# First two slots written from PSUM, relu and squares in tiles of their own, batch 1's softmax on VectorE in a fused three-layer kernel

## The chip, the cores and the metric

One Trainium2 chip, one of its cores. The metric is the device time of one execution in microseconds (us), lower is better; a page of the profile shows one profiled execution and its span. Engines by the names that the profile uses: PE (TensorE, with PEld for its weight loads), DVE (VectorE), ACT (ScalarE), POOL (GpSimd) and SP (SyncE, whose queue issues every DMA of this kernel).

## The reference

Two softmax attentions with shared values, then two feed-forward layers, all in float32.

```
def sm_attn(qq, kk, vv):                      # per batch (8) and head (8), head_dim 64
    a = softmax(qq @ kk.T / sqrt(64))
    return a @ vv
p_packed = sm_attn(p, k, v)                   # 32 packed rows from 576 tokens
x = sm_attn(q, p_packed, p_packed)            # 576 tokens, heads side by side: 512 wide
h = maximum(x @ w_in, 0)                      # 512 -> 2048
y = (h * h) @ w_out                           # 2048 -> 512
h = y @ w_in2                                 # 512 -> 1024
s = h * softmax(h)
out = layernorm(s) * g_ln @ w_out2            # 1024 -> 512, 4608 tokens
```

## The kernel before

Float32 products are made of pieces that TensorE takes at its faster float32r rate: a value is split into `hi` (a cast on ACT) and `lo` (value minus `hi`, on DVE or POOL, the helper `split_lo`), and each product runs as hi·hi, lo·hi and hi·lo.

**Packed attention, t = 0 to 9.** `Pack` handles four batches at once (`K0`: batches 0 to 3; batches 4 to 7 follow inside the main loop). Its results are `L[bg, k]` (packed values, hi and lo) and `slc`.

**The first weight is folded into the packed values.** x @ w_in equals a @ (p_packed @ w_in), head by head. So a `Unit(bg, s, g)` decodes a piece of w_in (s: one of eight column blocks of 512; g: half of the heads), and its `product` multiplies it with `L` for the four batches of group bg, into two PSUM banks named `pw`. ACT and DVE evict them (L320, L321) into the tile `pws`, and `store` writes it to DRAM (`pw_d`), one DMA per batch. `load_slot(b, s)` brings a batch's block back as `slot[b, s]`. For batch 0 and s below 2 there is a shortcut: `store` copies that batch's part of `pws` straight into the slot, four small DMAs per unit (`slot<-pws` in the profile), and three DMAs carry the other batches.

**The second softmax.** `s2_jobs(b, g)` is a list of jobs: scores on PE, 32x32 block transposes on DVE (`t`), row maximum, subtraction (L398), exp on ACT, sum, normalisation (L409), transpose back (`aT`, L414), and the split into `ah` and `al` (`at[b, g]`). `E` names the engine of the subtraction, the normalisation and `al`: DVE for batch 0, POOL for the others. Batch 0's second group runs at t = 9 in two halves of 288 tokens; batch 1 runs in the main loop, steps i = 1 to 5, four jobs in a step from the list `early[1]`, first all of group 0 and then all of group 1.

**The main loop, i = 0 to 255 (t = i + 10).** Step i runs `h1(i)`, six matmuls of a chunk of 128 columns of the first layer for 288 tokens: three with `at[b, 0]`, then three with `at[b, 1]`. ACT makes the relu r; the squares follow twice, once in full (`gg`, on ACT, or on POOL in part of the steps) and once as `hi` (`gh`, on ACT), and DVE makes `lo`: `gl` = gg - gh. Four steps later (three from i = 48) `ymm` runs twelve matmuls of the second product with gh and gl into four PSUM banks `Y`. Steps 0 to 3 and 4 to 7 are batch 0 with `slot[0, 0]` and `slot[0, 1]`; steps 8 to 15 are batch 1. r and gg are the two halves of one tile `rg`, of which there are two in turn:

```
        rg, g2 = t25("1", "rg"), t25("2", "ghl", F32R)
        r, gg, gh, gl = rg[:, :HF], rg[:, HF:S], g2[:, :HF], g2[:, HF:S]
        A.activation(r, pb[:, :HF], AF.Relu)
```

so the relu of step n is the first writer of the tile that step n - 2 used, and waits until all of step n - 2's readers are done, DVE's `gl` too.

**Who sets the order.** PE's matmuls and SP's DMAs are kept in program order (`pin`). DVE, ACT and POOL are ordered by a scheduler that plans ahead, except for the steps 138 to 245 (`strict`), where they too keep the order of the code; in those steps the kernel also decodes the weights of the last two layers (`raw`, `dw`, `op`) and prepares their left operands (`yf`, `yo`), and every ACT, DVE and POOL instruction shows line L53. Each engine runs its own list strictly in order. `later` is a list of DMAs put off to the next step; at the start of each step all of them are issued.

The last two layers run after step 249, by Strassen's scheme, with their own loop.

Of the kernel before, what the change touches and what calls it, by code (L numbers as in the profile page):

```python
# [12 lines left out]
F32R = mybir.dt.float32r  # L13
# [3 lines left out]
ALU = mybir.AluOpType  # L17
# [4 lines left out]
B, H, S, D, NPK = 8, 8, 576, 64, 32  # L22
# [3 lines left out]
HF = S // 2  # L26
# [6 lines left out]
def f(ap):  # L33
    return ap.bitcast(F32)


def build(tc, qT, kT, vP, pT, w_in, w_out, w_in2, w_out2, g_ln, out):
# [6 lines left out]
    pin = tc.keep_in_program_order  # L44
# [10 lines left out]
    V, A, G = Engine(nc.vector), Engine(nc.scalar), Engine(nc.gpsimd)  # L55

    def mm(*a, **k):
        pin(PE.matmul(*a, **k))  # L58
# [4 lines left out]
    def dma(out, in_):  # L63
        pin(SP.dma_start(out=out, in_=in_))
# [11 lines left out]
    pw_d = dr.tile([B, 8, P, 2, 512], F32, name="pw_d")  # L76
# [7 lines left out]
    def bank(name):  # L84
        return ps.tile([P, 512], F32, tag="a", name=name, bufs=4)
# [27 lines left out]
    def t25(k, name, dt=F32):  # L113
        return mp.tile([P, KC * P], dt, tag="e" + k, name=name, bufs=2 if k == "1" else 4)
# [47 lines left out]
    L, s1 = {}, {}  # L162
# [114 lines left out]
    wo, slot = {}, {}  # L277
    T0 = 10
    ring, clock = [0], [0]
    later, soons, lows = [], [], []  # L280
# [8 lines left out]
    class Unit:  # L289
# [14 lines left out]

        def product(self):
            bg, s, g = self.bg, self.s, self.g
            t = [bank("pw") for _ in range(2)]
            for j in range(2):
                c = slice(j * 256, (j + 1) * 256)
                for i, (a, x) in enumerate(((0, 0), (1, 0), (0, 1))):  # L310
                    for hh in range(2):
                        r = slice(64 * hh, 64 * hh + 64)
                        mm(t[hh][:, c], L[bg, 2 * g + j][r, a, :], self.w[r, x, c], start=(i == 0), stop=(i == 2))
            if bg == 0 and s < 2 and (0, s) not in slot:
                new_slot(0, s)
            sb = self.pl.tile([P, 4, 2, 2, P], F32R, tag="pws", name="pws", bufs=2)
            for hh in range(2):
                o = sb.rearrange("p (j h) c l x -> p h j c l x", h=2)[:, hh]
                src = t[hh].rearrange("p (j c x) -> p j c x", j=2, c=2)
                pin(A.copy(o[:, :, :, 0], src))  # L320
                V.tensor_tensor(out=o[:, :, :, 1], in0=src, in1=f(o[:, :, :, 0]), op=ALU.subtract)  # L321
            later.append(lambda: self.store(f(sb.rearrange("p h c l x -> p h (c l x)"))))

        def store(self, sf):
            bg, s, g = self.bg, self.s, self.g
            for b4 in range(4):
                r = slice(32 * b4, 32 * b4 + 32)
                if bg == b4 == 0 and s < 2:
                    o = f(slot[0, s].rearrange("p g c l x -> p g (c l x)"))
                    for h in range(4):  # L330
                        dma(o[32 * h:32 * h + 32, g], sf[r, h])
                else:
                    dma(pw_d[4 * bg + b4, s, :, g].rearrange("(h p) c -> p h c", h=4), sf[r])

    def new_slot(b, s):
        slot[b, s] = big4(ring[0], [P, 2, 2, 2, P], "slot", F32R)
        ring[0] += 1
# [17 lines left out]

    def s2_jobs(b, g, qf=None, parts=1):
        bg, b4 = divmod(b, 4)
        E = V if b == 0 else G
        st = {}

        def j_load():
            if qf:
                st["qf"] = qf
                return
            t = atB["p"].tile([P, 2, S], F32, tag="qf", name="qf", bufs=2)
            dma(t, qT[b, g])
            st["qf"] = [t[:, 0], t[:, 1]]

        def j_mm():
            st["t"] = atA.tile([P, 18, 32], F32, tag="t", name="t", bufs=3)  # L370
            st["mx"], st["sm"] = (atA.tile([P, 18], F32, tag=x, name=x, bufs=2) for x in ("mx", "sm2"))
            pb = [bank("s2") for _ in range(2)]
            for j in range(2):
                for k in range(2):
                    mm(pb[j][64 * k:64 * k + 64, :HF], slc[bg][:, 2 * g + k, b4, :],
                       st["qf"][k][:, j * HF:(j + 1) * HF], start=True, stop=True)
            st["pb"] = pb
            if b < 2:
                j_tr()

        def j_tr():
            for j in range(2):
                V.transpose(out=st["t"].rearrange("p n j -> p (n j)")[:, j * HF:(j + 1) * HF], in_=st["pb"][j][:, :HF])

        def part(p):
            n = 18 // parts
            r = slice(p * n, (p + 1) * n)
            c = slice(p * n * 32, (p + 1) * n * 32)
            t, mx, sm = (lambda: st["t"][:, r]), (lambda: st["mx"][:, r]), (lambda: st["sm"][:, r])

            def over(x):
                return x.unsqueeze(2).to_broadcast([P, n, 32])

            def j_max():
                V.tensor_reduce(out=mx(), in_=t(), op=ALU.max, axis=AX.X)

            def j_sub():
                E.tensor_tensor(out=t(), in0=t(), in1=over(mx()), op=ALU.subtract)  # L398

            def j_exp():  # L400
                A.activation(t(), t(), AF.Exp)

            def j_sum():
                V.tensor_reduce(out=sm(), in_=t(), op=ALU.add, axis=AX.X)
                V.tensor_scalar_add(sm(), sm(), 1e-9)
                V.reciprocal(sm(), sm())

            def j_norm():
                E.tensor_tensor(out=t(), in0=t(), in1=over(sm()), op=ALU.mult)  # L409

            def j_back():
                if p == 0:
                    st["aT"] = atA.tile([P, S], F32, tag="t", name="aT", bufs=3)
                V.transpose(out=st["aT"][:, c], in_=t().rearrange("p n j -> p (n j)"))  # L414

            def j_fin(c):
                def go():
                    if (b, g) not in at:
                        at[b, g] = [atp.tile([P, S], F32R, tag=f"a{x}{g}", name="a" + x, bufs=2) for x in "hl"]
                    hi, lo = at[b, g]  # L420
                    A.copy(hi[:, c], st["aT"][:, c])  # L421
                    soon(lambda: split_lo(E, lo[:, c], st["aT"][:, c], hi[:, c]))
                return go

            fins = [j_fin(c)] if parts == 2 else [j_fin(slice(0, HF)), j_fin(slice(HF, S))]
            return [j_max, j_sub, j_exp, j_sum, j_norm, j_back] + fins

        return [j_load, j_mm] + ([j_tr] if b > 1 else []) + [j for p in range(parts) for j in part(p)]


    gt = {}

    def h1(n):
        b, half, fc = n
        c = slice(half * HF, (half + 1) * HF)
        pb = bank("h1")
        w = slot[b, fc // 2][:, :, fc % 2]
        i = 0
        for g in range(2):
            ah, al = at[b, g]  # L440
            for l, x in ((0, ah), (1, ah), (0, al)):
                mm(pb[:, :HF], w[:, g, l], x[:, c], start=(i == 0), stop=(i == 5))
                i += 1
        rg, g2 = t25("1", "rg"), t25("2", "ghl", F32R)
        r, gg, gh, gl = rg[:, :HF], rg[:, HF:S], g2[:, :HF], g2[:, HF:S]
        A.activation(r, pb[:, :HF], AF.Relu)  # L446
        t = clock[0]

        def squares():
            if t < T0 + 20 or strict[0] and t % 2:  # L450
                A.activation(gg, r, AF.Square)
            else:
                G.tensor_tensor(out=gg, in0=r, in1=r, op=ALU.mult)  # L453
            A.activation(gh, r, AF.Square)

        gt[n] = (gh, gl)
        return squares, lambda: split_lo(V, gl, gg, gh)
# [76 lines left out]
    for b in range(2, B):  # L534
        base = (b - 1) * 32
        js = [s2_jobs(b, g) for g in range(2)]
        first, end = (15, 31) if b == 2 else (3, 26)
# [6 lines left out]
        for s in range(8):  # L544
            i = 16 + 2 * s + 3
            if b == 2:
                i = (17, 19, 21, 23, 25, 31, 33, 35)[s]
            if b == 4:
                i = max(i, 9 + 24 * s // 5)
# [122 lines left out]
    for n in range(8):  # L672
        i = P1 + 1 + PS * n
# [242 lines left out]
    for t in range(max(max(j for j in jobs if j != "first"), T0 + N + LAG - 1) + 2):  # L916
        i = t - T0
        clock[0] = t
        for fn in later:
            fn()  # L920
        later.clear()
        for n in ((0,), (1,), (2,), (3,), (4, 5), (6, 7))[t] if t < 6 else ():
            K0.load_v(n)
        if t + 3 < H:
# [26 lines left out]
        if t == 9:  # L951
            early[0] = s2_jobs(0, 1, q0[1], 2)
            for j in early[0][:2]:
                j()
            products()
            for j in early[0][2:9]:
                j()
            open_b()
            early[1] = s2_jobs(1, 0), s2_jobs(1, 1)
            for x in early[1]:  # L960
                x.pop(0)()
            early[1] = early[1][0] + early[1][1]
        strict[0] = R0 <= i < 246
        sq = None
        if 0 <= i < N:
# [146 lines left out]
```

## Time and profile before

| what | value |
|---|---|
| time, median of 3 runs | 1228.52 us (1227.23 to 1230.28) |
| the profiled execution: its time / its span | 1227.72 us / 1225.9 us |
| PE busy | 1146.4 us (94%) |
| DVE, ACT, POOL busy | 876.5, 662.4, 587.6 us (71, 54, 48%) |
| PE busy in 0 to 100, 100 to 200, 200 to 300 us | 63.52, 88.84, 97.11 us |
| PE busy in 600 to 700 us | 92.50 us, with DVE at 82.97 |

The time of an execution is 1.8 us above its span. PE is the engine with the most work; where its busy share falls, the row of the matmul that comes next says how long PE sat idle and what released it. The granted clock (PEclk) is a share of TensorE's full speed: 1.00 is 2.4 GHz, and the lower level, 1.2 GHz, would read 0.50.

### The profile page before, as it was taken

The page shows a single profiled execution, that of the slowest core. Times are in us where ns is not written, and L with a number is a line of the kernel's source. Part 1 is how long each engine was busy: PE and PEld are TensorE (multiplying, and loading weights), DVE is VectorE, ACT ScalarE, POOL GpSimd, SP SyncE. Part 2 cuts the span into 40 slices and gives each one's busy share as a digit, 9 for nine tenths or more (in the row PEclk, how much of TensorE's full clock was granted, in tenths as well). Part 3 has the DMA queues.
Part 4 walks back from the last instruction along what each step waited for, and adds up shares of the span by engine and source line. Part 5 has one row for each costly group of instructions (what it writes and reads, how often), then busy time and mean ns, then how long its engine had stood idle before and what let it go on. Part 6 is the DMA issues. An engine that isn't in the chain of part 4 may idle for free. (4 is left out here: it accounts for less than half of the span.)

```text
span 1225.9 us, 23705 instructions
## 1 busy us (share of the span) xinstructions
PE 1146.4 (94%) x8556; PEld 1057.7 (86%) x8556; DVE 876.5 (71%) x1688; ACT 662.4 (54%) x1501; POOL 587.6 (48%) x599
## 2 busy tenths in 40 slices
PE   6577899999999999999999899999999999999998
PEld 3366899898999998998998899998888889889897
DVE  4867488745326766578887973257989889889886
ACT  3465555344445555565666665435554655655553
POOL 1133255534225534486865762123744664745743
PEclk9888899999999999999999999999999999999999
DMA  9676697755155799789699799644142143223201
GB/s 332 209 215 189 189 270 246 239 197 204 60 196 147 209 292 291 215 307 356 229 386 337 249 341 366 226 167 150 35 151 82 36 151 101 89 83 108 78 23 48
DMA packets 125541, 239.06 MB, mean 195 GB/s; under 512 B 16880, under 2 KB 44528, under 8 KB 125424
## 3 DMA queue, kind: packets, MB, share of 16 engines
q1 hardware_dynamic: 125424, 237.55, 58.1%
q8 instruction: 67, 1.10, 0.4%
q14 instruction: 50, 0.41, 0.1%
HBM read 144.71 MB, written 91.75 MB: 193 GB/s over the span
## 5 line engine op out<-in xcount | busy, mean ns | idle before, releaser
L58 PE MATMUL Y<-ghl,woh 128*128 128x288 f32 x2048 | 471.1, 306 | 17.0 <-DVE ghl L53 7.2
L58 PEld LDWEIGHTS Y<-ghl,woh 128*128 128x128 f32 x2048 | 350.3, 192 | 32.3 <-DVE ghl L53 8.7
L58 PE MATMUL Y<-ghl,wol 128*128 128x288 f32 x1024 | 307.0, 300 | 0.0
L58 PE MATMUL h<-ah,slot 128*128 128x288 f32 x1024 | 217.2, 301 | 25.9 <-DMA slot<-pws 11.3
L58 PEld LDWEIGHTS Y<-ghl,wol 128*128 128x128 f32 x1024 | 197.2, 193 | 0.0
L822 PE MATMUL o<-wx,ch 128*128 128x256 f32 x1008 | 191.0, 286 | 5.0 <-DVE ys L839 3.0
L1016 POOL TENSOR_TENSOR cl<-raw,ch 128x512 fp32r<-128x512 f32 x100 | 148.2, 1500 | 96.6 <-ACT ch L1015 51.1
L58 PEld LDWEIGHTS h<-ah,slot 128*128 128x128 f32 x1024 | 168.5, 192 | 29.1 <-ACT ah L421 12.9
L453 POOL TENSOR_TENSOR rg<-rg 128x288 f32<-128x288 f32 x128 | 93.2, 729 | 182.5 <-ACT rg L446 171.6
L822 PEld LDWEIGHTS o<-wx,ch 128*128 128x128 f32 x1008 | 159.9, 192 | 11.8 <-DVE ys L839 4.4
L58 PE MATMUL h<-al,slot 128*128 128x288 f32 x512 | 152.6, 298 | 0.0
L822 PE MATMUL o<-wx,cl 128*128 128x256 f32 x504 | 142.9, 286 | 2.4 <-POOL cl L1016 1.9
L67 DVE TENSOR_TENSOR ghl<-rg,ghl 128x288 fp32r<-128x288 f32 x149 | 80.4, 545 | 87.7 <-POOL rg L453 58.8
L446 ACT ACTIVATE rg<-h 128x288 f32<-128x288 f32 x148 | 60.4, 408 | 107.8 <-PE h L58 105.2
L53 DVE TENSOR_TENSOR ghl<-rg,ghl 128x288 fp32r<-128x288 f32 x107 | 75.7, 719 | 51.2 <-ACT ghl L53 26.3
L1015 ACT CAST ch<-raw 128x512 fp32r<-128x512 f32 x126 | 76.8, 623 | 61.6 <-DVE raw L1021 53.8
L53 ACT ACTIVATE rg<-h 128x288 f32<-128x288 f32 x108 | 44.1, 408 | 110.5 <-PE h L58 56.2
L822 PEld LDWEIGHTS o<-wx,cl 128*128 128x128 f32 x504 | 96.0, 191 | 4.8 <-POOL cl L1016 2.9
L58 PEld LDWEIGHTS h<-al,slot 128*128 128x128 f32 x512 | 98.3, 192 | 0.4 <-POOL al L67 0.4
L67 POOL TENSOR_TENSOR ws<-dw,ws 128x512 fp32r<-128x512 f32 x32 | 41.9, 1309 | 98.5 <-ACT ws L298 85.0
L822 PE MATMUL h<-wi,y 128*128 128x512 f32 x312 | 83.5, 402 | 0.4 <-DVE hs L839 0.3
L1021 DVE TENSOR_TENSOR raw<-raw 128x512 f32<-128x512 f32 x70 | 74.2, 1069 | 9.9 <-POOL cl L1016 5.0
(166 smaller groups left out, 2118.0 us busy)
## 6 DMA issues: line engine op xcount, KB each, us to landing
pw_d<-pws SPq DMA_DIRECT2D x124, 256.0 KB, 4.4
slot<-pw_d SPq DMA_DIRECT2D x62, 512.0 KB, 6.1
yc_d<-yo SPq DMA_DIRECT2D x98, 256.0 KB, 6.0
y<-yc_d SPq DMA_DIRECT2D x92, 256.0 KB, 4.3
raw<-w_in SPq DMA_DIRECT2D x40, 512.0 KB, 6.4
raw<-w_out SPq DMA_DIRECT2D x24, 512.0 KB, 6.2
kf<-kT SPq DMA_DIRECT2D x32, 288.0 KB, 5.8
out<-ys SPq DMA_DIRECT2D x72, 128.0 KB, 1.7
```

The costliest lines, as they stand in the source:

```text
L53: return (lambda *a, **k: pin(fn(*a, **k))) if strict[0] else fn
L58: pin(PE.matmul(*a, **k))
L67: eng.tensor_tensor(out=lo, in0=x, in1=f(hi), op=ALU.subtract)
L446: A.activation(r, pb[:, :HF], AF.Relu)
L453: G.tensor_tensor(out=gg, in0=r, in1=r, op=ALU.mult)
L822: PE.matmul(bk, x, w[:, y], start=(i == 0), stop=(i == 3 * nk - 1))
L1015: A.copy(c[n][0], x)
L1016: eng.tensor_tensor(out=c[n][1], in0=x, in1=f(c[n][0]), op=ALU.subtract)
L1021: eng.tensor_tensor(out=out, in0=x, in1=y, op=op)
```

## The change

Five edits in one: (1) a new method `first` computes batch 0's part of a unit for s below 2 by itself, with twelve narrow matmuls into one more PSUM bank `pd`, and ACT and DVE write hi and lo from there into the slot; the four `slot<-pws` DMAs of each of the four units go. (2) The stores put off by `later` are held back during steps 1 to 3 and issued at step 4. (3) Batch 1's subtraction, normalisation and `al` go to DVE. (4) Batch 1's two groups are interleaved in `early[1]`. (5) r and gg get a tile each, for the whole loop, each with two halves in turn.

```
         def product(self):
             bg, s, g = self.bg, self.s, self.g
+            if bg == 0 and s < 2:
+                self.first()
...
-            if bg == 0 and s < 2 and (0, s) not in slot:
-                new_slot(0, s)
...
+        def first(self):
+            s, g = self.s, self.g
+            if (0, s) not in slot:
+                new_slot(0, s)
+            t = bank("pd")[:, :256]
+            for j in range(2):
+                for i, (a, x) in enumerate(((0, 0), (1, 0), (0, 1))):
+                    for hh in range(2):
+                        r = slice(64 * hh, 64 * hh + 64)
+                        mm(t[64 * j + 32 * hh:64 * j + 32 * hh + 32], f(L[0, 2 * g + j][r, a, :32]),
+                           f(self.w[r, x, j * 256:(j + 1) * 256]), start=(i == 0), stop=(i == 2))
+            o, src = slot[0, s][:, g], t.rearrange("p (c x) -> p c x", c=2)
+            pin(A.copy(o[:, :, 0], src))
+            V.tensor_tensor(out=o[:, :, 1], in0=src, in1=f(o[:, :, 0]), op=ALU.subtract)
...
         def store(self, sf):
-            for b4 in range(4):
+            for b4 in range(bg == 0 and s < 2, 4):
                 r = slice(32 * b4, 32 * b4 + 32)
-                if bg == b4 == 0 and s < 2:
-                    o = f(slot[0, s].rearrange("p g c l x -> p g (c l x)"))
-                    for h in range(4):
-                        dma(o[32 * h:32 * h + 32, g], sf[r, h])
-                else:
-                    dma(pw_d[4 * bg + b4, s, :, g].rearrange("(h p) c -> p h c", h=4), sf[r])
+                dma(pw_d[4 * bg + b4, s, :, g].rearrange("(h p) c -> p h c", h=4), sf[r])
...
-        E = V if b == 0 else G
+        E = V if b < 2 else G
...
-        rg, g2 = t25("1", "rg"), t25("2", "ghl", F32R)
-        r, gg, gh, gl = rg[:, :HF], rg[:, HF:S], g2[:, :HF], g2[:, HF:S]
+        if not rg:
+            rg.extend(t25("1", "rg") for _ in range(2))
+        g2 = t25("2", "ghl", F32R)
+        c = slice(rn[0] * HF, rn[0] * HF + HF)
+        rn[0] ^= 1
+        r, gg, gh, gl = rg[0][:, c], rg[1][:, c], g2[:, :HF], g2[:, HF:S]
...
-        for fn in later:
-            fn()
-        later.clear()
+        if not 1 <= i <= 3:
+            for fn in later:
+                fn()
+            later.clear()
...
-            early[1] = early[1][0] + early[1][1]
+            x, y = early[1]
+            early[1] = x[:4] + [j for z in zip(x[4:], y) for j in z] + y[len(x) - 4:]
```

The edits move instructions on the engines that a scheduler orders. First VectorE at t = 9, batch 0's second group (tiles `t` and `aT` of 288 columns, two halves). Before:

```order
L398 TENSOR_TENSOR t<-t,mx 128x288
L405 TENSOR_SCALAR sm_694<-sm_694 128x9
L406 RECIPROCAL sm_694<-sm_694 128x9
L409 TENSOR_TENSOR t<-t,sm_694 128x288
L404 TENSOR_REDUCE sm_694<-t 128x9
L414 STREAM_TRANSPOSE aT<-t 128x288
L321 TENSOR_TENSOR pws<-pw,pws 128x2x2x128
```

With the change:

```order
L409 TENSOR_TENSOR t<-t,mx 128x288 x2
L321 TENSOR_TENSOR pws<-pw,pws 128x2x2x128 x2
L141 TENSOR_SCALAR dw<-dw 128x512
L415 TENSOR_REDUCE sm_705<-t 128x9
L147 SCALAR_TENSOR_TENSOR dw<-raw,dw 128x512
...
L149 SCALAR_TENSOR_TENSOR dw<-raw,dw 128x512
...
L420 TENSOR_TENSOR t<-t,sm_705 128x288 x2
L425 STREAM_TRANSPOSE aT<-t 128x288 x2
```

The first half's transpose back (`aT`) now stands behind two `pws` evictions, a decode of three instructions (`dw`) and the second half's own work; before it stood ahead of them.

Next VectorE in steps 2 to 5, batch 1 (576 columns). Before, its last pieces there:

```order
L404 TENSOR_REDUCE sm_925<-t 128x18
L405 TENSOR_SCALAR sm_925<-sm_925 128x18
L406 RECIPROCAL sm_925<-sm_925 128x18
L67 TENSOR_TENSOR ghl<-rg,ghl 128x288
L414 STREAM_TRANSPOSE aT<-t 128x576
```

With the change, from the sum of the first group to the end of the second:

```order
L415 TENSOR_REDUCE sm_905<-t 128x18
L409 TENSOR_TENSOR t<-t,mx 128x576
...
L420 TENSOR_TENSOR t<-t,sm_905 128x576
L415 TENSOR_REDUCE sm_938<-t 128x18
...
L425 STREAM_TRANSPOSE aT<-t 128x576
...
L67 TENSOR_TENSOR al<-aT,ah 128x288 x2
...
L420 TENSOR_TENSOR t<-t,sm_938 128x576
...
L425 STREAM_TRANSPOSE aT<-t 128x576
```

The subtraction, the normalisation and `al` now stand in VectorE's own list, and the second group's steps follow the first group's at one place instead of a softmax later.

Last ScalarE in the strict steps, with the engines that an instruction waits for in brackets (names with h are step outputs in PSUM). Before:

```order
L53 ACTIVATE rg<-h_6359 128x288 [waits DVE_49,PE_49]
L53 ACTIVATE t<-t 128x576
L53 ACTIVATE ghl<-rg 128x288 [waits Activation_49]
L53 ACTIVATE rg<-h_6385 128x288 [waits DVE_49,PE_49]
L53 ACTIVATE t<-t 128x576 [waits Pool_49]
L53 ACTIVATE rg<-rg 128x288 [waits Activation_49]
```

With the change:

```order
L53 ACTIVATE rg<-h_6265 128x288 [waits PE_49,Pool_49]
L53 ACTIVATE t<-t 128x576
L53 ACTIVATE ghl<-rg 128x288 [waits Activation_49]
L53 ACTIVATE rg<-h_6290 128x288 [waits PE_49]
L53 ACTIVATE t<-t 128x576 [waits Pool_49]
L53 ACTIVATE rg<-rg 128x288 [waits DVE_49,Activation_49]
```

The order is the same; the relu (`rg<-h`) waits for VectorE no more, and in the steps where ACT makes the full square (`rg<-rg`) that wait now stands there, behind the instructions in between.

## Rows read from the trace of the kernel before

**Rows 1.** The page, part 1: busy time, share and instructions of each engine.
```profile
PE 1146.4 (94%) x8556; PEld 1057.7 (86%) x8556; DVE 876.5 (71%) x1688; ACT 662.4 (54%) x1501; POOL 587.6 (48%) x599
```

**Rows 2.** PE's waits in 0 to 250 us: total, times, longest.
```profile
PE h L58 <- DMA slot<-pws: 11.3, 2, 6.9
...
PE h L58 <- ACT ah L421: 5.6, 1, 5.6
```

**Rows 3.** PE's waits in 250 to 870 us.
```profile
PE Y L58 <- DVE ghl L53: 7.2, 4, 2.4
PE Y L58 <- ACT ys L53: 4.6, 3, 2.2
```

**Rows 4.** Busy us by stretch: PE, PEld, DVE, ACT, POOL, PEclk, DMA share, GB/s.
```profile
50.00:60.00 10.00, 5.01 (x26) 2.99 (x26) 9.45 (x22) 4.48 (x11) 2.54 (x2) 0.67 0.39 132
60.00:70.00 10.00, 7.63 (x50) 6.15 (x51) 8.49 (x17) 6.76 (x15) 2.60 (x2) 0.65 0.47 113
70.00:80.00 10.00, 5.58 (x31) 4.58 (x30) 3.09 (x6) 3.56 (x9) 2.31 (x2) 0.86 0.83 197
80.00:90.00 10.00, 8.86 (x59) 7.99 (x57) 8.27 (x12) 7.32 (x19) 4.51 (x4) 0.97 0.90 333
90.00:100.00 10.00, 4.92 (x23) 4.10 (x24) 8.75 (x13) 5.61 (x14) 6.20 (x6) 0.55 0.36 121
```

**Rows 5.** Timeline of PE: start, duration, instruction, idle before it and its releaser.
```profile
61.90 0.82 PE L58 MATMUL h<-ah,slot 128*128 128x288 f32 x2 [6.89 <-DMA slot<-pws]
...
76.77 0.50 PE L58 MATMUL h<-ah,slot 128*128 128x288 f32 x2 [4.42 <-DMA slot<-pws]
...
95.03 0.85 PE L58 MATMUL h<-ah,slot 128*128 128x288 f32 x2 [5.61 <-ACT ah L421]
...
137.96 0.82 PE L58 MATMUL h<-ah,slot 128*128 128x288 f32 x2 [5.14 <-DMA slot<-pw_d]
```

**Rows 6.** Timeline: transposes back of the second groups, batch 0 (first half) and batch 1.
```profile
56.79 0.47 DVE L414 STREAM_TRANSPOSE aT<-t 128x288 f32<-128x288 f32 x1
...
93.74 0.78 DVE L414 STREAM_TRANSPOSE aT<-t 128x576 f32<-128x576 f32 x1 [1.04 <-POOL t L409]
```

**Rows 7.** Timeline, 40 to 95 us: durations of the kinds that are added or moved.
```profile
42.17 0.75 DVE L398 TENSOR_TENSOR t<-t,mx 128x576 f32<-128x576 f32 x1
...
53.45 0.98 PE L58 MATMUL pw<-ws,L 64*128 64x256 f32 x12
...
59.98 0.68 DVE L147 SCALAR_TENSOR_TENSOR dw<-raw,dw 128x512 uint32<-128x512 uint32 x1
...
62.89 2.93 PE L58 MATMUL pw<-ws,L 64*128 64x256 f32 x24
...
89.19 1.65 DVE L149 SCALAR_TENSOR_TENSOR dw<-raw,dw 128x512 uint32<-128x512 uint32 x1
...
92.53 1.17 POOL L409 TENSOR_TENSOR t<-t,sm 128x576 f32<-128x576 f32 x1 [2.24 <-DVE sm L406]
```

**Rows 8.** Timeline of SP: the loads of batch 1's first two slots.
```profile
80.40 1.47 SPq L64 DMA_DIRECT2D slot<-pw_d  x2
```

**Rows 9.** ACT's wait of the strict steps in total; timeline of the strict steps.
```profile
ACT rg L53 <- DVE ghl L53: 51.4, 27, 4.2
...
561.63 0.30 PE L58 MATMUL h<-al,slot 128*128 128x288 f32 x1
...
564.70 0.41 ACT L53 ACTIVATE rg<-h 128x288 f32<-128x288 f32 x1 [3.87 <-DVE ghl L53]
...
567.67 0.40 PE L58 MATMUL Y<-ghl,woh 128*128 128x288 f32 x1 [2.25 <-ACT ys L53]
...
658.11 0.40 PE L58 MATMUL Y<-ghl,woh 128*128 128x288 f32 x1 [0.81 <-ACT ys L53]
...
686.34 0.54 PE L58 MATMUL Y<-ghl,woh 128*128 128x288 f32 x2 [2.25 <-DVE ghl L53]
```

**Rows 10.** Stretch behind the wait at 567.67, columns as in rows 4.
```profile
570.00:580.00 10.00, 10.00 (x68) 8.89 (x67) 7.37 (x14) 4.63 (x12) 4.40 (x6) 0.89 1.02 362
```

More of the change, by code (lines that the diff above doesn't have):

```diff
@@ L431, in build @@
     gt = {}
+    rg, rn = [], [0]
     def h1(n):
```

## The prediction

> **What bounds the kernel now.** I read the page first: PE is busy 94% of the span [rows 1], so a gain has to come out of the 80 us in which PE does not work, or out of matmuls that run at the lower clock. Then PE's waits, for two stretches. Up to 250 us the largest are 11.3 us for `slot<-pws`, two waits, and 5.6 us for batch 1's `ah` [rows 2]: both stand where the change edits. From 250 to 870 us PE waits 7.2 us for DVE's `gl` and 4.6 us for ACT's copies of Y [rows 3]: the stage that edit 5 reaches. Then the timeline at these waits [rows 5, 9], and the stretches around them for what else was busy [rows 4]. What the reader is to see there: from 50 to 60 us DVE is busy 9.45 of 10 us while PE idles half the time, from 70 to 80 us DVE has 3.09 us of work, and from 80 to 100 us it is full again. So the start is bound in turn by DVE (softmax of batch 0), by the small DMAs (steps 0 to 4), and by DVE with POOL (softmax of batch 1). PEclk is 0.65 at 60 to 70 us and 0.55 at 90 to 100 us: half of PE's idle time is paid a second time, since behind each long wait matmuls run at 1.2 GHz.
>
> All sums are made against the profiled execution: 1227.72 us, 0.8 us below the median of the three runs.
>
> **The start, step by step.**
>
> (a) *The wait of 6.89 us before 61.90.* Taking away the DMA alone would start PE earlier, since batch 0's first half of `aT` is transposed at 56.79 [rows 6]. But DVE's new list puts other work ahead of that transpose: two `pws` evictions of about 0.66 us each (such an eviction of 128x512 is like the decode op's 0.68 [rows 7]), the three decode ops (two at 0.68, one shorter, 0.4 estimated), the second half's sum and normalisation (288 columns, about 0.45 each, from 0.75 for 576 [rows 7] less a fixed part), small ops (0.35), and the new slot eviction (0.4, estimated as 256 columns against 512 at 0.66; bounds 0.3 and 0.66). That is 1.32 + 1.76 + 0.9 + 0.35 + 0.4 = 4.7 us, so `aT` ends at 57.26 + 4.7 = 62.0 instead of 57.26. PE's 24 narrow matmuls of the units (0, 0) and (0, 1) come on top: twelve `pw` matmuls take 0.98 us [rows 7], the narrow ones stream as many columns and I give them the same; the first twelve push batch 0's scores back by up to 1 us, the second twelve lie in PE's idle time. With the cast, PE resumes between 62.4 and 63.4 instead of 61.90. I take **+1.0 us** (0 to +2): the DMA's wait becomes a wait for DVE, and nothing is won here.
>
> (b) *24 more narrow matmuls* for the units (1, 0) and (1, 1), between step 0 and step 1. The 24 `pw` matmuls there take 2.93 us [rows 7], at PEclk 0.65; at full clock twice 0.98. I take **+2.9 us** (2.0 to 4: one more bank per unit out of four can make PE wait for an eviction, of which the nearest row is 0.66). Eviction itself is four ACT copies and four DVE subtractions of about 0.4 us, counted in (a) and (d).
>
> (c) *The wait of 4.42 us before 76.77* [rows 5]. Step 4 reads `slot[0, 1]`, which DVE now writes right behind the narrow matmuls, some 7 us earlier. **-4.4 us**, and behind it some 3 us at half clock (PEclk 0.86 at 70 to 80, 0.97 at 80 to 90 [rows 4]: 1.4 + 0.3 = 1.7 us lost), of which I take back 1.5. Step 8 would then be reached at its old place, about 88.8, + 1.0 + 2.9 - 4.4 - 1.5 = 86.8 us.
>
> (d) *The wait of 5.61 us before 95.03* for batch 1's second `ah`. Here the end is set by DVE's own list, which I add up from the end of batch 0's `aT` (62.4 to 63.4) to the end of batch 1's second `aT`. With 0.45 us for a `gl` or `al` of 288 columns, 0.48 for a block transpose of 288, 0.75 for 576 columns [rows 7], 0.68 for a decode op and 0.66 for an eviction: behind batch 0's softmax three decode ops, two `al`, one `gl` 3.2; four slot and `pws` groups 3.4; four block transposes 1.9; two maxima, subtractions, sums, normalisations 6.0; small ops 0.9; two `aT` 1.6; `al` 0.9; seven `gl` 3.2; six decode ops 3.6. Sum 24.7 us, so 87 to 88, and 1 to 2 us of waits for ACT's exp: `aT` ends at 88.5 to 90, against 93.74 + 0.78 = 94.5 before [rows 6]. Before, DVE had only 3.09 us of work from 70 to 80 us [rows 4], and behind that the chain took turns with POOL (the 1.17 us of L409 [rows 7], then the transpose). PE resumes at about 90 instead of 95.03: **-5.0 us** in all for (a) to (d), since PE, there at 86.8 + 0.6, waits for this anyway; (a), (b) and (c) are hidden in it as long as they bring PE there before 90. Bounds: if DVE gains nothing on POOL, 0; if its list runs without a gap, -6.5. A shorter wait (2.6 us) should leave less at half clock: 4.5 us are lost at PEclk 0.55 [rows 4], I take **-0.5**.
>
> Perfetto Trace Analysis in the Trainium skill (section Optimizing Scalar/DVE Operations) speaks against this edit: it advises moving work away from a saturated DVE, to GpSimd if need be, and adds that moving work between these two might not help because they share a port. The trace shows the sharing (a decode op of 0.68 us takes 1.65 at 89.19, while POOL runs) and so speaks for taking POOL's part away; by the page's rule alone term (d) would be 0, and the sum -4.5.
>
> (e) *The held-back stores and the loads behind them.* Per unit, SP issues three DMAs instead of seven. Batch 1's two slot loads went out at 80.40 [rows 8]; now four loads of weights and six stores stand ahead of them, the stores waiting for the last `pws` eviction (about 70, from the sum in (d)). At the 0.6 to 0.9 us per issue of SP's rows (1.47 for two [rows 8]) the loads go out at about 75. Step 8 needs them at 87, the cover is 12 us: 0. If that cover is gone, step 8 waits for the slot as step 18 does now (5.14 us [rows 5]).
>
> (f) *Behind 95 us.* Step 18's wait of 5.14 us hangs on a chain of product, store and load that moves along with PE: 0 (bounds -2 and +1).
>
> Start: -5.5 us, bounds -9 and +1.
>
> **Relu and squares apart.** Over the strict steps ACT waits 51.4 us in 27 places for DVE's `gl` of two steps before [rows 9]; ACT is not the bound, so what counts is where PE stood still behind it. At 564.70 a relu had waited 3.87 us; the last of PE's matmuls that it reads ended at 561.63 + 0.30 = 561.9 [rows 9], some 2.7 us earlier. ACT then works from 564.70 to the Y copies, and PE waits for these 2.25 us, until 567.67. With the relu freed the copies come 2.7 us earlier, and the whole wait goes: -2.25. PEclk behind it is 0.89 for 10 us [rows 10]: 1.1 us. The wait of 0.81 at 658.11 is of the same kind: -0.8. At 686.34 [rows 9] PE waits 2.25 us for DVE itself, whose list an earlier ACT can only shorten where it waits for ACT: I take -0.4, near the lower end. The other waits of this kind in [rows 3] count 0. Sum **-4.5 us**. Bounds: 0, if POOL's or ACT's full square, which now does the waiting, is late enough to bring the same waits back; and -11.8, both totals [rows 3], with some 4 us of clock behind them. Nothing can be later than before by this edit alone: each wait that is added was part of one that it replaces.
>
> **Sum.** 1227.7 - 5.5 - 4.5 = 1217.7; forecast **1218 us**.
>
> **The rivals.**
>
> *Half of it: only one of the two gains comes* (either the start is no better, because DVE ends batch 1 at 94 us as before, or the relu's wait only moves on to the square). For it: each rests on chains in which DVE is near full. 1222 to 1224 us. Chance 0.14.
>
> *More: both, and the later waits shrink as well.* In the strict steps a DVE that gets its operands earlier is also ahead at the waits for `gl`. With the bounds above, -9 and -9: 1205 to 1213. Chance 0.12.
>
> *No change.* The waits move on by one: 87 to 95 us filled by DVE, step 18's load later by what the start gained, the strict steps bound by DVE. 1225 to 1231. Chance 0.15.
>
> *Slower: VectorE becomes the bound of the first steps.* It takes over 4.8 us of POOL's work in a stretch where it is already at 8 to 9 tenths. Its price: the list in (d) has some 24.7 us; if a third of it runs at the 1.65 of the decode op beside POOL instead of 0.68, that is +11 us, batch 1 ends at 100, step 8 runs 5 us later than now, and with no gain behind 500 us the time is 1232 to 1234. It decides from the point where the second `aT` ends behind 94.5 us by more than the strict steps give back, about 99. Against it: POOL loses the eight ops of this softmax, so less runs beside DVE. Chance 0.09.
>
> **Chances and range.** Both gains about as summed (1213 to 1222): 0.50; the rivals as above. A measurement tells 0.3%, 3.7 us, from no change: faster 0.50 + 0.14 + 0.12 = 0.76, same 0.15, slower 0.09. The range 1209 to 1229 leaves out the lower half of "more" (0.06) and the upper end of "no change" with "slower" (0.13).
>
> **What would show it.** (a) PE's step 0 resumes at 62 to 64 us, released by ACT's `ah` and not by a DMA. (c) No wait before step 4. (d) The second `aT` of batch 1 ends at 88 to 90 us, and PE's first long wait behind 70 us ends at about 90. (e) The loads of batch 1's slots are issued at 74 to 77 us. Edit 5: ACT's waits for DVE's `gl` at relus vanish, those of the squares take at most half of the 51.4 us, and the waits at 567 and 658 are gone. The prediction is wrong if batch 1's `ah` comes after 94 us, if step 1 stalls for PSUM by more than 3 us, or if PE's total for `gl` and Y copies stays near 11.8 us.

## The result, and the profile after

| what | before | changed kernel |
|---|---|---|
| time, median of 4 runs each | 1227.88 us | **1216.45 us** (1212.41 to 1216.89) |
| ratio to before, 95% interval | | 0.9898 [0.9883, 0.9913] |
| span of the profiled execution | 1225.9 us | 1215.1 us |

The forecast was 1218 us, faster by over 0.3%: both held. The number came out well, in part by luck: of the reasons one was wrong, one edit was taken to be worth nothing and is worth something, and two terms were sized badly; the experiments below sort them. (One of the twelve executions of a kernel further down, the one with the interleave alone, took 2771.84 us, over twice the others, and is in no ratio.)

The page of the changed kernel, part 1, against [rows 1]:

```profile
PE 1148.2 (94%) x8652; PEld 1055.3 (87%) x8652; DVE 879.2 (72%) x1700; ACT 665.6 (55%) x1505; POOL 581.8 (48%) x591
```

PE has 96 more instructions and no less work, so the gain is idle time and clock, as it had to be. PE's waits in 0 to 250 us (total, times, longest), against [rows 2]:

```profile
PE h L58 <- ACT ah L432: 10.1, 2, 6.7
...
PE h L58 <- DMA slot<-pw_d: 4.4, 1, 4.4
```

The 11.3 us for `slot<-pws` are gone, but the waits for `ah` grew from 5.6 to 10.1 us. PE's timeline shows where, against [rows 5]:

```profile
62.50 0.85 PE L58 MATMUL h<-ah,slot 128*128 128x288 f32 x2 [6.68 <-ACT ah L432]
...
89.73 0.53 PE L58 MATMUL h<-ah,slot 128*128 128x288 f32 x2 [3.38 <-ACT ah L432]
...
91.64 0.61 PE L58 MATMUL h<-al,slot 128*128 128x288 f32 x1 [1.38 <-DVE al L67]
...
132.56 0.82 PE L58 MATMUL h<-ah,slot 128*128 128x288 f32 x2 [4.43 <-DMA slot<-pw_d]
```

Step 0 waits as long as before, with ACT's `ah` (and behind it DVE's `aT`) in the DMA's place. Step 4 waits no more. Batch 1's second `ah` lets PE go at 89.73 instead of 95.03. Then `al` is a new wait of 1.38 us. Busy us by stretch, columns as in [rows 4]:

```profile
70.00:80.00 10.00, 10.00 (x77) 8.18 (x78) 8.81 (x21) 7.62 (x18) 0.00 (x0) 1.00 0.88 240
80.00:90.00 10.00, 6.62 (x48) 6.19 (x46) 10.00 (x18) 9.08 (x26) 2.58 (x2) 1.00 0.28 95
90.00:100.00 10.00, 8.12 (x47) 6.94 (x47) 6.97 (x11) 4.73 (x11) 2.97 (x3) 0.66 0.25 87
```

From 70 to 80 us PE and DVE are full, or nearly, where they had 5.58 and 3.09 us of work. From 80 to 90 us DVE is busy 10.00 of 10 us, while POOL works 2.58 us: POOL's idle engine beside DVE's full one is the first hint of what was wrong in the reasons.

How far the change is ahead can be read off SP's stores of `y_d`, which follow the main loop. The first is issued at 252.10 before and at 247.53 after (4.6 us ahead), the one at 525.94 at 521.28 (4.7), the one at 745.25 at 734.50 (10.75), and the end is 10.8 us earlier. So the start gave 4.6 us and the strict steps 6.1; the last two layers nothing.

The strict steps: ACT's wait for `gl` in 500 to 850 us, against [rows 9], and PE's waits in 250 to 870 us, against [rows 3]:

```profile
ACT rg L53 <- DVE ghl L53: 4.5, 5, 2.1
```

```profile
PE Y L58 <- DVE ghl L53: 6.5, 4, 2.7
PE Y L58 <- DVE ys L53: 2.6, 2, 2.3
```

The 51.4 us of ACT are 4.5, and the 4.6 us that PE waited for ACT's Y copies have no row any more.

### The profile page after: what moved, and what is told of

It is laid out like the page before. It is cut to its first block, busy times and chain, and to the rows that moved or that the text cites. A ratio compares the mean times of both kernels' runs of the same rounds, so it can differ in the third digit from the quotient of the medians.

```text
span 1215.1 us, 24017 instructions
## 1 busy us (share of the span) xinstructions
PE 1148.2 (94%) x8652; PEld 1055.3 (87%) x8652; DVE 879.2 (72%) x1700; ACT 665.6 (55%) x1505; POOL 581.8 (48%) x591
## 5 line engine op out<-in xcount | busy, mean ns | idle before, releaser
L58 PE MATMUL h<-ah,slot 128*128 128x288 f32 x1024 | 215.7, 299 | 18.4 <-ACT ah L432 10.1
```

## The experiments

Each kernel is one of the two with one part changed. In the expectations, theory A is the prediction's account and the others are the rivals to it; the last three runs were made after the first eight, and name their theories themselves. What they move is read at two places: when PE resumes for batch 1's second `ah` (95.03 before, 89.73 after), and the first store of `y_d` (252.10 and 247.53). These are of one profiled execution each; a ratio is over several executions, against the kernel before, run beside it.

How far two such executions can differ by themselves is seen at step 0, which none of the edits to batch 1's softmax (3 and 4) is meant to reach. PE resumes there at 61.90 in the kernel before and at 60.28 in the one with the interleave alone, and at 60.76 to 63.79 in the nine kernels with slots from PSUM. A difference of 1 to 2 us at the first store is therefore not shown by one execution; where step 0 is off by as much, it is said. DVE, ACT and POOL are ordered by the scheduler anew for each kernel, so that an edit can move instructions elsewhere too; no run here holds their lists fixed.

### Relu and squares: one tile, and apart alone

The changed kernel with r and gg in one tile again:

```
-        r, gg, gh, gl = rg[0][:, c], rg[1][:, c], g2[:, :HF], g2[:, HF:S]
+        r, gg, gh, gl = rg[:, :HF], rg[:, HF:S], g2[:, :HF], g2[:, HF:S]
```

> The changed kernel with edit 5 undone: relu and full square share a tile again. Theory A (freed relus shorten ACT's and so PE's waits in the strict steps): it loses the 6.2 us that the changed kernel gains between 490 and 780 us, so about 1222.5 (1220 to 1224), with PE's wait for the Y copies near 565 us back and ACT waiting tens of us for DVE's gl at relus. Rival (the strict steps gained because everything reaches them earlier, not through the tiles): 1216 to 1218, and the lead over the kernel before still grows from 4.6 to 10.8 us.

Measured: 1223.14 us, ratio 0.9962 [0.9949, 0.9975]. ACT waits 51.8 us in 27 places for `gl` again. The stores of `y_d` stand 4.3 us ahead of before at the first one and 4.1 at the one at 745.25: the start's gain is kept and nothing is added.

The kernel before with edit 5 alone:

> The kernel before with edit 5 alone. Theory A: the start is as before, the strict steps gain 6 us, about 1221.5 (1220 to 1224). Rival: no change, 1226 to 1229.

Measured: 1221.56 us, 0.995 [0.9938, 0.9961]. The first store is at 251.54 (0.6 us ahead), the last one at 737.40 (7.9 ahead). Theory A's number: edit 5 is worth about 6 us by itself, and it and the start add up.

### Batch 1's softmax: on which engine, in which order

The changed kernel with `E = V if b == 0 else G` (edit 3 undone):

> The changed kernel with edit 3 undone: batch 1's subtraction, normalisation and al on POOL again, interleaved and with the slots from PSUM. Theory A (the start's end is set by the chain to batch 1's second transpose): the chain gets POOL's 1.17 us instead of 0.75 for two steps in each group and a hand-over at each, and al takes 1.0 instead of 0.4 us: PE resumes 2 to 4 us later than 89.7, about 1219 (1217.5 to 1221). Rival B (the start's gain comes from the slots written from PSUM): 1216 to 1217.5.

Measured: 1214.14 us, 0.9897 [0.9883, 0.9911]: not slower, and below either theory's range. PE's timeline, and the stretch of 80 to 90 us:

```profile
87.35 0.53 PE L58 MATMUL h<-ah,slot 128*128 128x288 f32 x2 [0.62 <-ACT ah L432]
```

```profile
80.00:90.00 10.00, 7.90 (x57) 7.14 (x55) 9.97 (x14) 8.35 (x24) 8.03 (x8) 1.00 0.28 97
```

With the softmax on POOL, PE resumes 2.4 us **earlier** than with it on DVE. DVE is still full in this stretch and POOL is busy 8.03 of 10 us: the two groups' chains run side by side on two engines. Theory A fails here.

The changed kernel with `early[1] = early[1][0] + early[1][1]` (edit 4 undone, still on DVE):

> The changed kernel with edit 4 undone: batch 1's groups one after the other, on DVE. Theory A: group 1 gets to DVE one to two steps later, its transpose ends 2 to 5 us behind 89.2, about 1219.5 (1218 to 1222). Rival B: 1216 to 1217.5.

Measured: 1216.92 us, 0.9909 [0.9896, 0.9922].

```profile
93.97 0.85 PE L58 MATMUL h<-ah,slot 128*128 128x288 f32 x2 [5.99 <-ACT ah L432]
```

PE resumes 4.2 us later, as theory A has it, but the time lies in rival B's range and cannot be told from the change's 0.9898. In this execution PE was late already at step 0 (63.79 against 62.50).

Both edits undone (slots from PSUM, stores held and edit 5 stay):

> The changed kernel with edits 3 and 4 undone: slots from PSUM, stores held, r and gg apart, batch 1's softmax on POOL and its groups in turn. If the interleave is what gains the start (first theory): PE resumes at 96 to 98 behind a wait of 8 us or more, and the time is that of edit 5 alone, 1221 to 1222.5 us. If the held stores already bring the softmax forward by themselves (second theory): PE resumes at 92 to 93, 1218.5 to 1220 us.

Measured: 1222.56 us, 0.9948 [0.9929, 0.9967], that of edit 5 alone. The first theory's numbers.

```profile
96.83 0.85 PE L58 MATMUL h<-ah,slot 128*128 128x288 f32 x2 [9.62 <-ACT ah L432]
```

The four together, all with the other edits in:

| batch 1's softmax | step 0 | PE resumes | first `y_d` | median |
|---|---|---|---|---|
| POOL, groups in turn | 62.47 | 96.83 | 254.27 | 1222.56 |
| DVE, groups in turn | 63.79 | 93.97 | 249.78 | 1216.92 |
| POOL, interleaved | 62.71 | 87.35 | 245.63 | 1214.14 |
| DVE, interleaved (the change) | 62.50 | 89.73 | 247.53 | 1216.45 |

Read by the first store, DVE in place of POOL gives 4.5 us while the groups run in turn (5.8 counted from step 0), which fits a chain that need not change engines. The interleave gives 8.6 us on POOL (8.9 from step 0). On top of the interleave, DVE costs 1.9 us (2.1). On DVE the interleave gives 2.3 us, of which only 1.0 are left when counted from step 0. The medians of the last two rows don't tell them apart (the intervals of their ratios are nearly the same); a pair further down does.

The kernel before with the interleave alone:

```
-            early[1] = early[1][0] + early[1][1]
+            x, y = early[1]
+            early[1] = x[:4] + [j for z in zip(x[4:], y) for j in z] + y[len(x) - 4:]
```

> The kernel before with edit 4 alone (batch 1's two groups interleaved, still on POOL, slots by DMA, stores not held, r and gg in one tile). If the interleave alone brings the second `ah` forward (first theory): PE resumes about 90 instead of 95.03, the store of the first y_d at about 249 instead of 252.10, 1225 to 1226.5 us. If the interleave needs the slots from PSUM and the held stores (second theory): the two waits of about 7 and 4.5 us before 77 stay and the slot loads at about 80 end last, PE resumes at 92 or later, 1227 to 1229 us.

Measured: 1225.32 us, 0.9976 [0.9964, 0.9988], as the first theory has it. PE's timeline:

```profile
75.30 0.82 PE L58 MATMUL h<-ah,slot 128*128 128x288 f32 x2 [4.57 <-DMA slot<-pws]
...
88.02 0.50 PE L58 MATMUL h<-ah,slot 128*128 128x288 f32 x2 [0.76 <-ACT rg L446]
```

The two DMA waits stay, yet the wait for batch 1's second `ah` is gone, and the first store is 3.8 us ahead (248.28). Of these, 1.6 us were there before the interleave could act, since step 0 began that much earlier (60.28 against 61.90):

```profile
60.28 0.82 PE L58 MATMUL h<-ah,slot 128*128 128x288 f32 x2 [6.11 <-DMA slot<-pws]
```

That leaves 2.2 us, and 2.6 is what the medians show. So the interleave gains on POOL and without the slots too, though less than the 8.6 us that it gives with slots from PSUM and held stores.

### Slots and held stores

The changed kernel without the hold (`if not 1 <= i <= 3:` taken out):

> The changed kernel with edit 2 undone: the stores of the units (1, 0) and (1, 1) are issued at step 1, ahead of four loads of weights. Theory A: the loads go out some 5 to 9 us later (behind the last pws eviction at 72.8), but they are decoded only from step 4 on: 1216 to 1218, no change. Rival (the hold is what keeps the decode on time): DVE's decode and with it batch 1's second transpose move back by 3 us or more, 1219 to 1222.

Measured: 1218.01 us, 0.992 [0.9903, 0.9937]. SP's timeline, and PE's:

```profile
57.61 18.28 SPq L64 DMA_DIRECT2D pw_d<-pws  x9
75.94 1.16 SPq L64 DMA_DIRECT2D raw<-w_out  x1
```

```profile
92.87 0.53 PE L58 MATMUL h<-ah,slot 128*128 128x288 f32 x2 [3.40 <-ACT ah L432]
```

SP issues in order. Not held, the stores stand in its queue from 57.61 until the last `pws` is evicted, and the loads of weights behind them go out from 75.94 to 78.85, where the change issues them from 59.11 to 65.02. ACT's decode op of such a load stands ahead of its exp of the second group, and waits for the load; DVE waits 1.81 us behind it:

```profile
82.01 0.66 ACT L136 ACTIVATE dw<-raw 128x512 f32<-128x512 f32 x1 [1.78 <-DMA raw<-w_out]
```

`ah` comes 3.1 us later than in the change. Of these, DVE was 1.3 us behind before that wait (the second group's maximum at 77.72 against 76.44), where PE had a lower clock from 60 to 70 us (0.53 against 0.67); the kernel with r and gg in one tile, whose stores are held, had the same (0.54) and resumed at 90.84. So some 1.8 to 2.0 us are the hold's. The first store is at 251.29, 3.8 us behind the change, and 2.5 us are left at the store of 734.50. The rival's mechanism is seen, but the time lies at theory A's upper end, and its interval overlaps that of the change: in the time, the hold's worth is not shown.

The changed kernel with slots by DMA and no hold (edits 1 and 2 undone):

> The changed kernel with edits 1 and 2 undone: batch 0's slots go through pws and DMAs again, batch 1's softmax stays on DVE and interleaved. Theory A: a wait of some 4 us before step 4 comes back, but the chain on DVE to batch 1's second transpose still decides: DVE has 1.7 us less to do, PE 4 us of narrow matmuls less, so 1216 to 1219. Rival B (the slots are what gains): the start's whole gain goes, 1220.5 to 1222.

Measured: 1220.76 us, 0.9939 [0.9922, 0.9957]; first store 249.79. The waits of step 0 and step 4 are back (6.88 and 4.52 us), and PE resumes at 90.43, but now for batch 1's slot:

```profile
90.43 0.50 PE L58 MATMUL h<-ah,slot 128*128 128x288 f32 x2 [1.71 <-DMA slot<-pw_d]
```

Theory A's time is missed; rival B's is met, though by the first store half of the start's lead is still there (2.3 of 4.6 us). With the runs above, this sorts what the start needs, all with edit 5 in:

| slots from PSUM, stores held | softmax on DVE, interleaved | ratio to before |
|---|---|---|
| no | no | 0.995 [0.9938, 0.9961] |
| yes | no | 0.9948 [0.9929, 0.9967] |
| no | yes | 0.9939 [0.9922, 0.9957] |
| yes | yes (the change) | 0.9898 [0.9883, 0.9913] |

Neither pair of edits alone gains anything that its interval shows; both together gain 0.5%. PE needs its own way to step 8 and batch 1's `ah` to come earlier, and whichever is left late sets the time.

The kernel before with slots from PSUM alone (edit 1):

> The kernel before with edit 1 alone: slots from PSUM, no hold, softmax of batch 1 on POOL and in turn, one rg tile. Theory A: the wait before step 4 goes, and PE then waits longer for batch 1's second ah: 1226 to 1229. Rival B: 1222 to 1224.5.

Measured: 1229.11 us, 1.001 [0.9997, 1.0023]. Step 4 no longer waits, and step 8 waits for all of it:

```profile
96.77 0.85 PE L58 MATMUL h<-ah,slot 128*128 128x288 f32 x2 [9.86 <-ACT ah L432]
```

A transfer taken off the path gained nothing by itself here, since a later wait (for `ah`) then took all of the time.

### Beyond the change

The changed kernel with batch 0's fourth slot (s = 3) from PSUM as well, so that step 18's wait for its load has nothing to wait for:

```
-            if bg == 0 and s < 2:
+            if bg == 0 and s in (0, 1, 3):
                 self.first()
...
-            for b4 in range(bg == 0 and s < 2, 4):
+            for b4 in range(bg == 0 and s in (0, 1, 3), 4):
...
-        if i:
+        if i and s != 3:
```

> The changed kernel with one edit more: the slot [0, 3] from PSUM too, for the wait of 4.43 us before 132.56. Its cost is 24 narrow matmuls, 2 us at full clock, and four evictions of 0.4 us. If that wait goes with the half-clock stretch behind it (PEclk 0.66 at 130 to 140, about 3 us) and no wait for PSUM takes its place: 1211 to 1214. If step 18 only waits for the next thing (the evictions of pw, or batch 0's slot 2): 1215 to 1219.

Measured: 1214.0 us, 0.9887 [0.987, 0.9904]. The wait of 4.43 us at 132 is gone; new waits of 0.50, 1.31 and 0.85 us, for a relu and for evictions, stand between 113 and 119. First store 244.29, 3.2 us ahead of the change. The intervals of the two ratios overlap, so the times alone do not show this gain.

The same with the softmax on POOL:

> The changed kernel with batch 1's softmax back on POOL and slot [0, 3] taken from PSUM too. If the two gains are of different places and add (first theory: 2.3 us from POOL by the run with the softmax on POOL, 2.5 us from the slot by the run with the third slot): 1211 to 1212.5 us, PE resumes for batch 1's second `ah` at about 87.4 and no wait of 4 us for the load of slot [0, 3] at about 130. If both gain the same time, which a later wait then takes back (second theory): 1213.5 to 1214.5, and a wait for an eviction between 110 and 150 that neither run alone shows.

Measured: **1209.5 us** (1208.44 to 1210.21), 0.9841 [0.9824, 0.9858], the fastest version here and better than either theory's number. PE resumes at 87.91, and the waits between 113 and 119 are those of the run before. Against that run, which has the softmax on DVE, the intervals do not overlap: with the groups interleaved, POOL is the better place, by 0.46%.

That it gives more than the sum of the two is for the most part the clock. The stretches of 110 to 140 us with the softmax on POOL and two slots from PSUM, and then with three:

```profile
110.00:120.00 10.00, 7.58 (x48) 7.24 (x49) 7.06 (x13) 5.87 (x13) 2.68 (x3) 0.83 0.83 254
120.00:130.00 10.00, 6.51 (x49) 6.27 (x47) 5.82 (x11) 6.74 (x17) 2.56 (x2) 0.94 0.97 274
130.00:140.00 10.00, 8.75 (x51) 8.78 (x52) 2.71 (x5) 4.84 (x13) 0.31 (x1) 0.72 0.53 195
```

```profile
110.00:120.00 10.00, 7.34 (x67) 5.81 (x66) 6.95 (x11) 5.83 (x14) 3.22 (x3) 1.00 0.79 247
120.00:130.00 10.00, 10.00 (x77) 10.00 (x76) 6.86 (x12) 7.94 (x22) 1.95 (x2) 1.00 0.97 265
130.00:140.00 10.00, 10.00 (x81) 9.70 (x80) 5.59 (x11) 7.05 (x18) 3.89 (x4) 1.00 0.51 186
```

With two slots the clock falls to half twice, from 115 us on and from 129. The second fall begins inside the wait that ends at 131.25, where it costs nothing, as the stretch of 129 to 130 shows (PE busy 0.00, PEclk 0.50):

```profile
129.00:130.00 1.00, 0.00 (x0) 0.00 (x0) 0.00 (x0) 0.00 (x0) 0.00 (x0) 0.50 1.03 371
```

Counted only where PE works, 1.7 us of full speed are lost behind 115 and 2.2 behind 131; with three slots nothing is lost from 110 to 140. The waits of 2.42 (for `pws` at 115.11) and 4.74 us (for the load at 131.25) go; 2.7 us of waits between 113 and 119 and 48 narrow matmuls (two units, 2.15 + 1.95 = 4.1 us) come: 2.4 + 4.7 + 3.9 - 2.7 - 4.1 = 4.2 us. Measured are 5.0, from 1.5 us behind at a matmul of Y (99.56 against 98.07) to 3.5 ahead at another (169.03 against 172.53). The lead at the first store is 6.0 us (239.67 against 245.63): from 172 us on another 0.9 come from a wait for a relu that shrinks (1.02 to 0.17), and 1.7 from the clock at 220 to 230 us (0.83 with two slots, 1.00 with three). With three slots and the softmax on DVE such drops remain (0.91 and 0.92 at 110 to 130, 0.83 at 220 to 230), which only the two edits together avoid. Of the 6.0 us, 3.4 are left at the end of the span. The clock's part is read from one execution of each kernel.

## Why the prediction was right, and where it was not

**(a), the wait at 61.90.** Right. DVE's new list was summed to end `aT` at 62.0, and PE to resume at 62.4 to 63.4 behind ACT's `ah`. The changed kernel's DVE and PE: both halves' transposes end at 61.52 + 0.83 = 62.35, and PE resumes at 62.50. The difference from before is +0.6 us (+1.0 predicted), less than step 0 moves by itself between executions.

```profile
61.52 0.83 DVE L425 STREAM_TRANSPOSE aT<-t 128x288 f32<-128x288 f32 x2
```

**(b), the narrow matmuls.** Mis-sized. I counted twelve instructions to a unit, as the code writes them; the trace has 24 to a unit (96 for four units). The operands go through `f`, as plain float32, where the `pw` matmuls are float32r; that this is why was not tried. The two units between step 0 and step 1 took 3.21 and 1.95 us, 5.2 in place of 2.9. It did not show in the sum, since PE still got to step 8 early enough to wait (at 89.73 - 3.38 = 86.35, predicted 86.8).

**(c), the wait at 76.77.** Right: gone, and PEclk is 1.00 from 70 to 90 us.

**(d), the wait at 95.03.** The number was right, the reason wrong. `aT` was to end at 88.5 to 90 and PE to resume at about 90; it ended at 88.45 + 0.76 = 89.2, and PE resumed at 89.73. Even this sum came out by two errors that cancel: from 62.35 to 89.21 us DVE works 22.8 us, not 24.7, and waits 4.1 us, not 1 to 2, nearly all of it before 72.7 us for ACT's halves of the evictions and for `gh`, and not for exp. Further, I put this down to DVE doing POOL's part, so that the chain no longer "took turns with POOL", and gave as bounds 0 if DVE gains nothing on POOL and -6.5 if its list runs without a gap. With POOL doing its part, interleaved, PE resumes at 87.35: 7.7 us earlier than before, beyond the better bound. The step that failed is that I summed DVE's list for the two edits together and never for edit 4 alone. With the softmax on POOL, the second group's maximum comes at 85.85 on DVE in turn, and at 76.55 interleaved:

```profile
85.85 0.74 DVE L406 TENSOR_REDUCE mx<-t 128x18 f32<-128x576 f32 x1
```

```profile
76.55 0.74 DVE L406 TENSOR_REDUCE mx<-t 128x18 f32<-128x576 f32 x1
```

The gap between engines that I saw in [rows 6] was the consequence of one chain alone on two engines, and a second chain fills it.

I also wrote that (a), (b) and (c) are hidden in (d). The table of the section on the slots shows that (d) needs them: with the softmax edits but without slots and hold, the ratio is 0.9939 against 0.995 for edit 5 alone, and the intervals overlap.

The rule of the Trainium skill that the prediction set against this edit (Perfetto Trace Analysis, Optimizing Scalar/DVE Operations) was borne out in part. Interleaved, DVE saturated at 10.00 of 10 us is the wrong place for more work, by 1.9 us at the first store. With the groups in turn, taking the work from POOL to DVE gained 4.5 us, against its caution that moving between these two might not help.

**(e), the held-back stores.** The loads of batch 1's slots were issued at 75.16 (predicted 75), and step 8 did not wait for them. But I costed the hold only as a risk, 0. In the traces it has a value: without it the weights' loads go out 14 to 17 us later, ACT waits 1.78 us for one of them, and the first store is 3.8 us later. In the time it is 0.22%, between the ratios 0.992 and 0.9898, whose intervals overlap.

**(f), step 18.** 4.43 us in place of 5.14, within the bounds. That PE could be rid of it was not in the prediction; in the run with a third slot from PSUM this was worth 3.2 us at the first store.

**The start** gave 4.6 us, -5.5 predicted. PE was 5.3 us ahead when it resumed; the 1.38 us for `al` that nobody expected take part of it back. DVE's list has a decode op in front of that `al`, and it is a slow one:

```profile
88.45 0.76 DVE L425 STREAM_TRANSPOSE aT<-t 128x576 f32<-128x576 f32 x1
89.15 1.35 DVE L141 TENSOR_SCALAR dw<-dw 128x512 uint32<-128x512 uint32 x1
```

**Relu and squares apart** gave 6.1 us, -4.5 predicted: the mechanism was right and the size off. PE's idle time from 500 to 800 us, before and after:

```profile
500.00:800.00 300.00, 286.87 (x2068) 280.75 (x2067) 205.88 (x306) 177.00 (x477) 181.58 (x209) 0.98 0.84 303
```

```profile
500.00:800.00 300.00, 289.36 (x2089) 282.15 (x2088) 214.91 (x321) 179.79 (x478) 181.85 (x207) 0.99 0.83 301
```

That is 13.1 against 10.6 us, 2.5 less, somewhat under the 3.4 of waits that I added up; the waits for `gl`, of which I took 0.4 off the one at 686, shrank by 0.7 (7.2 to 6.5), and waits for DVE's Y copies grew from 1.3 to 2.6. In this pair the rest is the clock, for which I took 1.1 us behind one wait. The stretches in which it fell most, before and after:

```profile
560.00:570.00 10.00, 7.75 (x54) 6.88 (x53) 9.86 (x14) 5.91 (x17) 6.99 (x8) 0.94 0.77 296
570.00:580.00 10.00, 10.00 (x68) 8.89 (x67) 7.37 (x14) 4.63 (x12) 4.40 (x6) 0.89 1.02 362
...
620.00:630.00 10.00, 7.63 (x47) 7.40 (x47) 7.92 (x12) 6.53 (x18) 6.82 (x9) 0.84 1.02 390
650.00:660.00 10.00, 9.19 (x56) 8.31 (x57) 8.33 (x17) 7.65 (x22) 4.68 (x6) 0.83 1.03 368
700.00:710.00 10.00, 7.47 (x43) 7.01 (x42) 9.90 (x17) 6.68 (x20) 6.84 (x9) 0.83 0.61 200
```

```profile
640.00:650.00 10.00, 7.44 (x43) 6.65 (x43) 9.86 (x17) 8.25 (x24) 7.31 (x9) 0.83 1.04 392
690.00:700.00 10.00, 7.70 (x47) 7.45 (x47) 9.17 (x17) 5.64 (x18) 6.45 (x8) 0.83 0.58 169
```

Before, the clock dropped four times in 500 to 800 us (0.6 + 1.1 + 1.6 + 1.7 + 1.7 = 6.7 us lost), after twice (3.4): 3.3 us. With the 2.5 us of idle time that is 5.8 of the 6.1. Another pair of executions divides it otherwise. The changed kernel with r and gg in one tile:

```profile
500.00:800.00 300.00, 283.90 (x2052) 276.84 (x2052) 206.55 (x307) 176.83 (x476) 180.63 (x207) 0.99 0.84 301
```

It has 16.1 us of idle time and two drops of the clock (0.83 at 560 to 570 and at 680 to 690, 3.4 us), as many as the change: here 5.5 us of the gain are idle time and none is clock. The two terms together are alike (5.8 and 5.5 us), and it is their sum that the prediction made too small, 4.5; whether by the idle time or by the clock term, for which I looked behind one wait only, differs from one execution to the next and stays open. That the new wait of the squares would not bring the old one back was right (4.5 us in 5 places, not half of 51.4).

**The rivals.** *Half*: not so, both gains came. *More*: not with this change; its range is reached, at 1209.5, by undoing edit 3 and adding a slot. (Its second -9 is not the bound that was worked out for the strict steps, -11.8.) *No change* had the right mechanism for the slots alone (1.001), where the wait moves on to step 8. *VectorE becomes the bound of the first steps*: it does, from 80 to 90 us, but ends `aT` at 89.2 and not at 100; only two of its instructions there ran at the slow speed beside POOL (1.56 us at 85.33, 1.35 at 89.15), not a third of the list, since POOL had 2.58 us of work.

## What to carry to other kernels

When several edits meet at one wait, sum the list for each edit alone as well as for all: here the forecast was right for the sum, and the edit that it was credited to cost time. Where two paths end at one wait, expect little from shortening one: either pair of the start's edits (1 with 2, 3 with 4) gained nothing that the runs show, and all four gained 0.5%. Here a chain that hops between two engines was helped more by a second independent chain beside it (8.6 us) than by moving it to one engine (4.5 us). And a wait on PE can cost its own length and the clock behind it: list all places where the granted clock falls in the stage, count the loss only where PE works, and compare more than one pair of executions.

## What was not expected of the hardware

A decode op with a single tile as input (`tensor_scalar` on 128x512 integers) takes 0.42 us with POOL idle, and 1.35 us at 89.15 while POOL works on `ws`; the subtraction for `gl`, with two inputs, goes from 0.45 to 1.56 us at 85.33 beside POOL's `wol`:

```profile
85.05 1.52 POOL L67 TENSOR_TENSOR wol<-dw,woh 128x512 fp32r<-128x512 f32 x1 [17.89 <-ACT woh L358]
88.94 1.27 POOL L67 TENSOR_TENSOR ws<-dw,ws 128x512 fp32r<-128x512 f32 x1 [2.36 <-issue]
```

Both began after POOL's instruction and ended 0.3 us after it: 90.50 against 90.21, and 86.89 against 86.57. So do three more decode ops of this kind in the same trace, at 57.46, 62.27 and 110.95 (0.28 us after POOL's each): the later one looks as if it waited for the other's end, and was not slowed evenly. The Trainium skill's page SBUF — State Buffer (Who interferes with whom) says that a DVE instruction with two SBUF inputs contends with a GpSimd one that reads SBUF, which the second agrees with; the first it allows for only in some faster modes, and no run here shows which mode this op was in. Both engines gained from working at once all the same: with DVE and POOL at 9.97 and 8.03 of 10 us (softmax on POOL), the second `aT` began at 86.07, against 88.45 with DVE at 10.00 and POOL at 2.58.
